# A spectral-filter and MLP kernel: first batch by halves of d, second transpose stored by halves, last output tiles in banks of their own

## The chip, the cores and the metric

The kernel runs on one core of a Trainium2 chip. The metric is device time in microseconds (us), the median of several executions. The kernel before took 802.25 us (4 runs, 801.14 to 803.52).

Names of engines in the profile: PE is the matrix engine (TensorE), PEld its weight load, DVE the vector engine, ACT the scalar engine, POOL is GpSimd, SP issues output stores. PSUM is the memory into which this kernel's matmuls write. The granted clock is PE's clock as the profile shows it, 1.00 being full speed.

## The reference

Eight batches of 3008 tokens with 256 channels (d) are filtered in the frequency domain, then go through a two-layer MLP.

```python
def _attn_ref(x, filt_r, filt_i):            # x: (8, 3008, 256)
    X = np.fft.rfft(x, axis=1)
    Y = X * (filt_r + 1j * filt_i)[None]
    return np.fft.irfft(Y, n=x.shape[1], axis=1)

def _moe_ref(x, w_in, w_out):                # x: (24064, 256), w_in: (256, 2048)
    h = x @ w_in
    return np.maximum(0.01 * h, h) @ w_out
```

## The kernel before

The Fourier transform of length 3008 is split as 94 x 32. Each batch passes through six stages:

- S1: 32 matmuls with a weight each, from x; ACT (and DVE, in batch 0) copies the results out of PSUM.
- T1: four DVE transposes of 32x32 blocks.
- S2: matmuls with a fixed weight; the filter is multiplied on DVE and GpSimd.
- SA: the inverse of S2; ACT copies.
- T2: four DVE transposes again.
- SB: 64 small matmuls, the inverse of S1; copies into `yt`, the MLP's input.

The MLP works on chunks of 512 tokens, each in eight slots. In one slot PE does four matmuls of layer one (`moe1_group`), then spectral tasks of the next batch (`tasks`), then half an output tile of the chunk before (`moe2_slice`). Batch 0 has no MLP to hide behind: its stages are the head of the kernel.

```python
    x_load(0, 4)                       # x of batch 0: four quarters of n2, all of d
    for c0 in (0, HC):                 # filters: two halves of their 24 columns, all of d
        filt_load(fa_sb, filt_r, c0, c0 + HC)
        filt_load(fb_sb, filt_i, c0, c0 + HC)
    ...
    def turn(src, dst, i, flat):       # T1 and T2, part i of 4
        ...
        o = dst[:].bitcast(FP32).rearrange("p (n e) -> p e n", n=Q)[:, ts(i, w), :]
        nc.vector.transpose(o, a)
    ...
    po_ps = pop.tile([P, 2, D], FP32, name="po_ps")   # both output tiles in one PSUM bank
    def moe2_slice(ci, g):
        po = po_ps[:, tj % 2, :]
        ...                            # 8 matmuls into po
        nc.scalar.copy(osts[ci][:, tj % 2, :], po)
        ...                            # one store for two tiles
    ...
    for g in range(16):                # the head, in program order
        s1_group(0, g, two[(g // 2) % 2], copies[g % 2])()
    ...
    upper(fa_sb, 0, HC)                # ACT copies the filter to partitions 64..127
    upper(fb_sb, 0, HC)
    for i in range(4):
        t1_part(0, i)()
    ...                                # S2, filter, SA
    E1 = 6
    for g in range(E1):                # six S1 groups of batch 1, ahead of the MLP
        s1_group(1, g, two[g % 2])()
    for i in range(4):
        t2_part(0, i)()
    for g in range(16):
        sb_group(0, g, copies[g % 2 if g >= 8 else 0], two[(g // 2) % 2])()
    ...
    plan(1, 0, E1, 3, 4, 9, 4, 3, 24, 30)   # slots of batch 1's stages beside the MLP
```

The arguments of `plan` are the batch, the slot of its first S1 group, the first S1 group still to do, S1 groups per slot, the slots where T1 and S2 begin, S2's step, SA's lag, and the slots where T2 and SB begin.

## Time and profile before

The trace splits into three stretches. The MLP begins at 54.71 us, its last layer-one group at 785.55, and the span ends at 800.8.

| stretch, kernel before | us | what it is |
|---|---|---|
| start to first MLP matmul | 54.71 | head: batch 0's chain |
| first to last layer-one group | 730.84 | middle: PE full from about 75 us |
| from there to the end | 15.25 | tail: last output tiles and stores |

Such a table comes from the timeline alone: one looks for the first and the last matmul of a kind.

### The profile page before, as it was taken

The numbers are of one execution on the slowest core, as the hardware profiler recorded it, in microseconds if no ns is written. First come the engines' busy times: TensorE is split into PE (matmuls) and PEld (weight loads), VectorE is DVE, ScalarE is ACT, GpSimd is POOL, SyncE is SP. The second block draws the span as 40 slices with busy tenths as digits, with TensorE's granted clock in tenths as the row PEclk, the third lists the DMA queues.
The fourth block names the chain that finished last, engine by engine and source line by source line (L and its number), as shares of the span: only waits on it lengthen the run. The fifth ranks groups of instructions, "written<-read, shape, count | busy, mean of one in ns | idle before, by whom it ended". The sixth has DMA issues, their size and how long they took to land. (4 is left out here: it accounts for less than half of the span.)

```text
span 800.8 us, 13437 instructions
## 1 busy us (share of the span) xinstructions
PE 764.3 (95%) x5708; PEld 525.5 (66%) x5708; DVE 362.0 (45%) x450; ACT 565.6 (71%) x803; POOL 154.0 (19%) x137
## 2 busy tenths in 40 slices
PE   3668999999999999999999999999999999999997
PEld 2144667766776667866678667776677666776665
DVE  4547852477307743186524773077432765200000
ACT  4767767877686776977678776877768776666663
POOL 6672500052002400034000520024000340000000
PEclk9889999999999999999999999999999999999999
DMA  9934010501014101230105010141100101110011
GB/s 197 173 51 91 27 40 28 117 27 40 27 38 108 40 27 40 63 82 28 40 27 118 27 41 27 40 105 41 41 27 27 41 27 41 40 41 35 32 40 53
DMA packets 32027, 43.14 MB, mean 54 GB/s; under 512 B 2262, under 2 KB 30038, under 8 KB 31310
## 3 DMA queue, kind: packets, MB, share of 16 engines
q0 software_dynamic: 5664, 15.99, 11.2%
q1 hardware_dynamic: 26160, 25.53, 9.0%
q8 instruction: 44, 0.72, 0.4%
q10 hardware_dynamic: 144, 0.77, 0.3%
q14 instruction: 15, 0.12, 0.0%
HBM read 33.64 MB, written 24.64 MB: 73 GB/s over the span
## 5 line engine op out<-in xcount | busy, mean ns | idle before, releaser
L287 ACT ACTIVATE gt_c<-h_c_g 128x1024 f16<-128x1024 f32 x376 | 385.4, 1026 | 193.9 <-PE h_c_g L282 192.9
L293 PE MATMUL po_ps<-w_out_sb,gt_c 128*128 128x256 f16 x3008 | 389.1, 272 | 2.5 <-ACT ost_c_t L299 2.5
L282 PE MATMUL h_c_g<-yt,w_in_sb 128*128 128x512 f16 (+7 forms) x1728 | 386.6, 351 | 1.5 <-ACT gt_c L287 1.3
L293 PEld LDWEIGHTS <-gt_c 128*128 128x128 f16 x3008 | 290.6, 98 | 91.1 <-issue 6.3
L282 PEld LDWEIGHTS <-w_in_sb 128*128 128x128 f16 x1728 | 163.0, 98 | 97.1 <-issue 2.9
L184 DVE STREAM_TRANSPOSE big<-big 128x1024 f32<-128x1024 f32 x64 | 113.8, 1884 | 175.1 <-ACT big L175 175.0
L212 POOL TENSOR_TENSOR y_b_g<-p_b_g,p_b_g 128x512 f16<-128x512 f32 x84 | 106.9, 1273 | 222.3 <-DVE p_b_g L210 222.3
L261 DVE CAST yt<-sb_b_g 128x376 f16<-128x376 f32 x116 | 58.4, 545 | 93.2 <-PE sb_b_g L258 93.2
L299 ACT COPY ost_c_t<-po_ps 128x256 f32<-128x256 f32 x188 | 70.8, 377 | 17.1 <-PE po_ps L293 14.0
L208 DVE TENSOR_TENSOR p_b_g<-s_b_g,fa_sb 128x512 f32<-128x512 f32 x84 | 58.1, 692 | 37.2 <-PE s_b_g L198 34.6
L175 ACT CAST big<-s_b_g 128x512 f16<-128x512 f32 x120 | 65.8, 613 | 9.7 <-PE s_b_g L165 9.7
L122 POOL DMA_DIRECT2D x_sb<-in_x_dram x22 | 11.9, 548 | 271.9 <-PE s_b_g L165 265.5
L175 ACT CAST big<-sa_b_g 128x512 f16<-128x512 f32 x96 | 57.1, 602 | 2.3 <-PE sa_b_g L243 2.1
L209 DVE TENSOR_TENSOR p_b_g<-s_b_g,fb_sb 64x512 f32<-64x512 f32 x84 | 58.2, 693 | 1.1
L210 DVE TENSOR_TENSOR p_b_g<-s_b_g,fb_sb 64x512 f32<-64x512 f32 x84 | 57.4, 683 | 1.1
L165 PE MATMUL s_b_g<-x_sb,f_sb 94*128 94x256 f16 x256 | 41.6, 289 | 10.5 <-DMA x_sb<-in_x_dram 8.8
L243 PE MATMUL sa_b_g<-y_b_g,small_sb 128*128 128x512 f16 x108 | 40.6, 407 | 4.4 <-ACT big L175 4.1
L258 PEld LDWEIGHTS <-big 128*128 128x128 f16 x512 | 30.4, 103 | 19.5 <-DVE big L184 6.0
L165 PEld LDWEIGHTS <-f_sb 94*128 94x128 f16 x256 | 25.1, 102 | 23.0 <-issue 13.7
L258 PE MATMUL sb_b_g<-i_sb,big 128*128 128x94 f16 x512 | 33.9, 213 | 5.7 <-DVE big L184 5.6
L198 PE MATMUL s_b_g<-big,small_sb 128*128 128x512 f16 x84 | 31.8, 379 | 1.4 <-DVE big L184 1.4
L243 PEld LDWEIGHTS <-small_sb 128*128 128x128 f16 x108 | 11.0, 102 | 20.2 <-issue 8.6
(26 smaller groups left out, 86.9 us busy)
## 6 DMA issues: line engine op xcount, KB each, us to landing
out_dram<-ost_c_t SPq DMA_DIRECT2D x94, 256.0 KB, 2.1
x_sb<-in_x_dram POOLq DMA_DIRECT2D x7, 1024.0 KB, 8.6
x_sb<-in_x_dram POOLq DMA_DIRECT2D x7, 480.0 KB, 10.0
x_sb<-in_x_dram POOLq DMA_DIRECT2D x4, 256.0 KB, 7.9
w_in_sb<-in_moe_w_in_dram POOLq DMA_DIRECT2D x1, 1024.0 KB, 9.2
w_out_sb<-in_moe_w_out_dram POOLq DMA_DIRECT2D x1, 1024.0 KB, 9.6
f_sb<-fwd_const SPq DMA_DIRECT2D x4, 192.0 KB, 4.5
fa_sb<-in_filt_r_dram POOLq DMA_DIRECT2D x8, 96.0 KB, 7.1
```

Of the source, the lines that this page charges most:

```text
L165: nc.tensor.matmul(ps[:, j, :], f1_sb[:N1, n2, :], x_sb[:N1, n2, :], start=True, stop=True)
L175: copy(paired(dst)[:, ds(2 * g, 2)], ps[:].rearrange("p n (e t) -> p n e t", t=2))
L184: nc.vector.transpose(o, a)
L208: nc.vector.tensor_tensor(p1[:], ps[:], fa, AL.mult)
L209: nc.vector.tensor_tensor(p2[0:64], ps[64:P], fb[64:P], AL.mult)
L212: nc.gpsimd.tensor_tensor(y1[:], p1[:], p2[:], AL.add)
L258: nc.tensor.matmul(ps[:, j, :], src[:, n2, ts(dt, P // 2)], i1_sb[:, n2, :], start=True, stop=True)
L261: copy(yv[:, :, ds(4 * h, 4)], ps[:].rearrange("p c a -> p a c"))
L282: nc.tensor.matmul(ph[:, j, ds(o, ln)], w_in_sb[:, dt, ts(ct, P)], yts[b % 2][:, dt, ds(lo, ln)], start=(dt == 0), stop=(dt == NDT - 1),)
L287: nc.scalar.activation(gts[ci][:, ds(2 * g, 2), :], ph[:], AF.Lrelu)
L293: nc.tensor.matmul(po, gts[ci][:, ct, ts(tj, P)], w_out_sb[:, ct, :], start=(ct == 0), stop=(ct == NCT - 1))
L299: nc.scalar.copy(osts[ci][:, tj % 2, :], po)
```

## The change

Its intent is a shorter head and tail. Batch 0 is loaded and transformed in two halves of d (128 channels each), so that the second half's load lies beside the first half's work. T2 stores each half of d as a block, so that SB of the first half need not wait for T2's last two parts. The last chunk's output tiles get PSUM banks of their own and a store each. The early S1 groups of batch 1 are dropped, and in batch 1 T1 is planned two slots later and the stages after it one slot later.

```diff
-    x_load(0, 4)
-    for c0 in (0, HC):
-        filt_load(fa_sb, filt_r, c0, c0 + HC)
-        filt_load(fb_sb, filt_i, c0, c0 + HC)
+    for hf in range(2):
+        for n0 in (0, N2 // 2):
+            x_load(0, n0, N2 // 2, hf * DH, DH)
+        filt_load(fa_sb, filt_r, hf * DH, DH)
+        filt_load(fb_sb, filt_i, hf * DH, DH)
+    nc.gpsimd.dma_start(i1_sb[:], i1_d.ap())
+    nc.gpsimd.dma_start(w_in_sb[:], ...)
 ...
+    def t2_part(b, i):
 ...
+            o = big[(4 * b + 3) % 3][:].bitcast(FP32).rearrange("p (h n e) -> p h e n", h=2, n=Q)
+            nc.vector.transpose(o[:, i // 2, ts(i % 2, E4), :], a)
 ...
+    def upper(hf):       # real filter on ACT, imaginary on DVE
+        for t, cp in ((fa_sb, nc.scalar.copy), (fb_sb, nc.vector.tensor_copy)):
+            cp(t[64:P, :, ts(hf, DH)], t[0:64, :, ts(hf, DH)])
+    ac = (nc.scalar.copy, nc.scalar.copy)
+    first_front(0, copies)                  # S1 and T1 of half 0
+    upper(0)
+    first_s2(0, 0, False), first_s2(0, 1, True)    # True: the product is GpSimd's
+    first_s2(0, 2, False)
+    first_sa(0, 0, ac)
+    first_front(1, ac)                      # S1 and T1 of half 1, all copies on ACT
+    x_load(1)
+    first_sa(0, 2, ac), first_sa(0, 1, ac)
+    upper(1)
+    first_s2(1, 0, False), first_s2(1, 1, True)
 ...
-    plan(1, 0, E1, 3, 4, 9, 4, 3, 24, 30)
+    plan(1, 0, 0, 3, 6, 10, 4, 3, 25, 31)
 ...
+        last = ci == NCHUNK - 1
+        if last and half == 0:
+            pos[ci] = pfp.tile([P, D], FP32, tag="pf", name=f"o_c{ci}_t{tj}")[:]
+        po = pos[ci] if last else po_ps[:, tj % 2, :]
 ...
+        if last:
+            nc.sync.dma_start(out[ds(t0, P), :], ost[:, tj % 2, :])
```

More of the change, by code (lines that the diff above doesn't have):

```diff
@@ L115, with x_load, rows, filt_load @@
     fwd2, inv2, inv2x = (small_sb[:, i, :] for i in range(3))
-    def x_load(b, parts=1):
-        step = N2 // parts
+    DH = D // 2
+    def x_load(b, n0=0, nn=N2, d0=0, dn=D):
         src = x[b].rearrange("(n1 n2) d -> n1 n2 d", n2=N2)
-        for i in range(parts):
-            for lo, cnt in ((0, 64), (64, N1 - 64)):
-                nc.gpsimd.dma_start(
-                    x_sb[lo : lo + cnt, ts(i, step), :], src[lo : lo + cnt, ts(i, step), :]
-                )
-    def rows(src, first, pstep, cstep, np_, nc_):
+        for lo, cnt in ((0, 64), (64, N1 - 64)):
+            nc.gpsimd.dma_start(x_sb[lo : lo + cnt, ds(n0, nn), ds(d0, dn)],
+                                src[lo : lo + cnt, ds(n0, nn), ds(d0, dn)])
+    def rows(src, first, pstep, cstep, np_, nc_, d0, dn):
         return bass.AP(
-            tensor=src.tensor, offset=src.offset + first * D,
-            ap=[[pstep * D, np_], [cstep * D, nc_], [1, D]],
+            tensor=src.tensor, offset=src.offset + first * D + d0,
+            ap=[[pstep * D, np_], [cstep * D, nc_], [1, dn]],
         )
-    def filt_load(dst, src, c0, c1):
+    def filt_load(dst, src, d0, dn):
         h = N2 // 2
@@ L136, in filt_load @@
             nc.gpsimd.dma_start(
-                dst[q : q + h, c0:c1], rows(src, NC * s + c0, N1, 1, h, c1 - c0))
+                dst[q : q + h, :, ds(d0, dn)], rows(src, NC * s, N1, 1, h, NC, d0, dn))
             nc.gpsimd.dma_start(
-                dst[q + h : q + Q, c0:c1], rows(src, N1 - NC * s - c0, N1, -1, h, c1 - c0))
-    HC = NC // 2
+                dst[q + h : q + Q, :, ds(d0, dn)], rows(src, N1 - NC * s, N1, -1, h, NC, d0, dn))
     step = N2 // FP
@@ L147 @@
     nc.sync.dma_start(small_sb[:], small_d.ap())
-    x_load(0, 4)
-    for c0 in (0, HC):
-        filt_load(fa_sb, filt_r, c0, c0 + HC)
-        filt_load(fb_sb, filt_i, c0, c0 + HC)
+    for hf in range(2):
[4 more added lines that the diff above has]
+    nc.gpsimd.dma_start(i1_sb[:], i1_d.ap())
+    nc.gpsimd.dma_start(w_in_sb[:], moe_w_in.rearrange("(dt p) c -> p dt c", p=P))
     one = cpool.tile([1, 1], FP32, name="one")
@@ L157, with s1_group @@
     nc.vector.memset(big[2][:].rearrange("p (e n t) -> p e n t", n=Q, t=2)[:, :, NC:Q, :], 0.0)
-    def s1_group(b, g, pool=(pfp, "pf"), copy=nc.scalar.copy):
+    def s1_group(b, g):
         def go():
-            ps = pool[0].tile([P, 2, D], FP32, tag=pool[1], name=f"s1_b{b}_g{g}")
+            ps = pfp.tile([P, 2, D], FP32, tag="pf", name=f"s1_b{b}_g{g}")
             for j in range(2):
@@ L166, in go @@
                                  start=True, stop=True)
-            spread(big[(4 * b) % 3], g, ps, copy)
+            spread(big[(4 * b) % 3], 2 * g, ps, nc.scalar.copy)
         return go
@@ L172, in paired, with spread, t1_part, go @@
         return t[:].rearrange("p (e n t) -> p n e t", n=Q, t=2)
-    def spread(dst, g, ps, copy):
-        copy(paired(dst)[:, ds(2 * g, 2)], ps[:].rearrange("p n (e t) -> p n e t", t=2))
-    def turn(src, dst, i, flat):
-        w = D // 2 // 4
-        a = src[:].bitcast(FP32)[:, ts(i, w * Q)].rearrange("p (e n) -> p e n", n=Q)
-        if flat:
-            o = dst[:].bitcast(FP32)[:, ts(i, w * Q)].rearrange("p (e n) -> p e n", n=Q)
-        else:
-            o = dst[:].bitcast(FP32).rearrange("p (n e) -> p e n", n=Q)[:, ts(i, w), :]
-        nc.vector.transpose(o, a)
-    def turned(t, flat):
-        if flat:
-            return paired(t)
-        return t[:].rearrange("p (n e t) -> p n e t", n=Q, t=2)
-    def t1_part(b, i):
-        return lambda: turn(big[(4 * b) % 3], big[(4 * b + 1) % 3], i, b == 0)
+    def spread(dst, n0, ps, copy, e0=0):
+        nn, de = ps.shape[1], ps.shape[2] // 2
+        copy(paired(dst)[:, ds(n0, nn), ds(e0, de)], ps[:].rearrange("p n (e t) -> p n e t", t=2))
+    E4 = D // 2 // 4
+    def t1_part(b, i, flat=False):
+        def go():
+            a = big[(4 * b) % 3][:].bitcast(FP32)[:, ts(i, E4 * Q)].rearrange("p (e n) -> p e n", n=Q)
+            o = big[(4 * b + 1) % 3][:].bitcast(FP32)
+            if flat:
+                o = o[:, ts(i, E4 * Q)].rearrange("p (e n) -> p e n", n=Q)
+            else:
+                o = o.rearrange("p (n e) -> p e n", n=Q)[:, ts(i, E4), :]
+            nc.vector.transpose(o, a)
+        return go
+    def t2_part(b, i):
+        def go():
+            a = big[(4 * b + 2) % 3][:].bitcast(FP32)[:, ts(i, E4 * Q)].rearrange("p (e n) -> p e n", n=Q)
+            o = big[(4 * b + 3) % 3][:].bitcast(FP32).rearrange("p (h n e) -> p h e n", h=2, n=Q)
+            nc.vector.transpose(o[:, i // 2, ts(i % 2, E4), :], a)
+        return go
     ys = {}
-    def s2_mm(b, c, ps):
-        src = turned(big[(4 * b + 1) % 3], b == 0)
-        nc.tensor.matmul(ps.rearrange("p n (e t) -> p n e t", t=2), fwd2, src[:, ds(c, 2)],
-                         start=True, stop=True)
     def s2_group(b, g):
@@ L203, in go @@
             ps = pfp.tile([P, 2, D], FP32, tag="pf", name=f"s2_b{b}_g{g}")
-            s2_mm(b, 2 * g, ps[:])
+            src = big[(4 * b + 1) % 3][:].rearrange("p (n d) -> p n d", n=Q)
+            nc.tensor.matmul(ps[:], fwd2, src[:, ds(2 * g, 2), :], start=True, stop=True)
             fa, fb = fa_sb[:, ds(2 * g, 2), :], fb_sb[:, ds(2 * g, 2), :]
@@ L212, in go @@
             nc.gpsimd.tensor_tensor(y1[:], p1[:], p2[:], AL.add)
-            ys[(b, g)] = (y1[:],)
+            ys[(b, g)] = y1
         return go
-    def s2_wide(b, g, on_pool):
-        ps = php.tile([P, 4, D], FP32, tag="ph", name=f"s2_b{b}_w{g}")
-        for j in range(2):
-            s2_mm(b, 4 * g + 2 * j, ps[:, ds(2 * j, 2), :])
-        if on_pool:
-            xs = [scrp.tile([P, 2, D], FP32, tag=f"p{j + 1}", name=f"x_b{b}_w{g}_{j}") for j in range(2)]
-            y1 = outp.tile([P, 4, D], FP16, tag="ost", name=f"y1_b{b}_g{g}")
-            y2 = outp.tile([P, 4, D], FP16, tag="ost", name=f"y2_b{b}_g{g}")
-            for j in range(2):
-                nc.scalar.copy(xs[j][:], ps[:, ts(j, 2), :])
-            for y, f in ((y1, fa_sb), (y2, fb_sb)):
-                for j in range(2):
-                    nc.gpsimd.tensor_tensor(y[:, ts(j, 2), :], xs[j][:], f[:, ds(4 * g + 2 * j, 2), :], AL.mult)
-        else:
-            y1 = ypp.tile([P, 4, D], FP16, tag="yw1", bufs=2, name=f"y1_b{b}_g{g}")
-            y2 = ypp.tile([P, 4, D], FP16, tag="yw2", bufs=2, name=f"y2_b{b}_g{g}")
-            nc.vector.tensor_tensor(y1[:], ps[:], fa_sb[:, ts(g, 4), :], AL.mult)
-            nc.vector.tensor_tensor(y2[:], ps[:], fb_sb[:, ts(g, 4), :], AL.mult)
-        for j in range(2):
-            ys[(b, 2 * g + j)] = (y1[:, ts(j, 2), :], y2[:, ts(j, 2), :])
     def sa_group(b, g):
         def go():
-            y = ys.pop((b, g))
             ps = pfp.tile([P, 2, D], FP32, tag="pf", name=f"sa_b{b}_g{g}")
-            for i, (m, t) in enumerate(zip((inv2, inv2x), y)):
-                nc.tensor.matmul(ps[:], m, t, start=(i == 0), stop=(i == len(y) - 1))
-            spread(big[(4 * b + 2) % 3], g, ps, nc.scalar.copy)
-        return go
-    def t2_part(b, i):
-        return lambda: turn(big[(4 * b + 2) % 3], big[(4 * b + 3) % 3], i, False)
+            nc.tensor.matmul(ps[:], inv2, ys.pop((b, g))[:], start=True, stop=True)
+            spread(big[(4 * b + 2) % 3], 2 * g, ps, nc.scalar.copy)
+        return go
     def sb_group(b, g, copy, pool=(pfp, "pf")):
@@ L253, in go @@
         def go():
-            src = turned(big[(4 * b + 3) % 3], False)
+            src = big[(4 * b + 3) % 3][:].rearrange("p (h n d) -> p h n d", h=2, n=Q)
             ps = pool[0].tile([P, 4, N1], FP32, tag=pool[1], name=f"sb_b{b}_g{g}")
@@ L257, in go @@
                 n2 = 4 * h + j
-                nc.tensor.matmul(ps[:, j, :], src[:, n2, ts(dt, P // 2)], i1_sb[:, n2, :],
+                nc.tensor.matmul(ps[:, j, :], src[:, dt, n2, :], i1_sb[:, n2, :],
                                  start=True, stop=True)
@@ L262, in sb_group, with first_s1 @@
         return go
-    gts, osts = {}, {}
+    two = ((pfp, "pf"), (php, "ph"))
+    copies = (nc.scalar.copy, nc.vector.tensor_copy)
+    W = 8
+    def first_s1(hf, g, pool, copy):
+        ps = pool[0].tile([P, 4, DH], FP32, tag=pool[1], name=f"f1_h{hf}_g{g}")
+        for j in range(4):
+            n2 = 4 * g + j
+            nc.tensor.matmul(ps[:, j, :], f1_sb[:N1, n2, :], x_sb[:N1, n2, ts(hf, DH)],
+                             start=True, stop=True)
+        spread(big[0], 4 * g, ps, copy, hf * DH // 2)
@@ new lines, in first_s2 @@
+    def first_s2(hf, g, on_pool):
+        ps = php.tile([P, W, DH], FP32, tag="ph", name=f"f2_h{hf}_g{g}")
+        src = paired(big[1])
+        for j in range(2):
+            nc.tensor.matmul(ps[:, ts(j, 4), :].rearrange("p n (e t) -> p n e t", t=2), fwd2,
+                             src[:, ds(W * g + 4 * j, 4), ts(hf, DH // 2)], start=True, stop=True)
+        fs = [f[:, ts(g, W), ts(hf, DH)] for f in (fa_sb, fb_sb)]
+        if on_pool:
+            xs = [scrp.tile([P, 4, DH], FP32, tag=f"p{j + 1}", name=f"fx_h{hf}_g{g}_{j}") for j in range(2)]
+            y = [outp.tile([P, W, DH], FP16, tag="ost", name=f"fy{i}_h{hf}_g{g}") for i in range(2)]
+            for j in range(2):
+                nc.scalar.copy(xs[j][:], ps[:, ts(j, 4), :])
+            for i in range(2):
+                for j in range(2):
+                    nc.gpsimd.tensor_tensor(y[i][:, ts(j, 4), :], xs[j][:], fs[i][:, ts(j, 4), :], AL.mult)
+        else:
+            y = [ypp.tile([P, W, DH], FP16, tag=f"yw{i}", bufs=2, name=f"fy{i}_h{hf}_g{g}") for i in range(2)]
+            for i in range(2):
+                nc.vector.tensor_tensor(y[i][:], ps[:], fs[i], AL.mult)
+        ys[(hf, g)] = y
@@ new lines, in first_sa, with first_front @@
+    def first_sa(hf, g, cps):
+        y = ys.pop((hf, g))
+        for j in range(2):
+            ps = pfp.tile([P, 4, DH], FP32, tag="pf", name=f"fa_h{hf}_g{g}_{j}")
+            for i, m in enumerate((inv2, inv2x)):
+                nc.tensor.matmul(ps[:], m, y[i][:, ts(j, 4), :], start=(i == 0), stop=(i == 1))
+            spread(big[2], W * g + 4 * j, ps, cps[j], hf * DH // 2)
+    def first_front(hf, cps):
+        for g in range(8):
+            first_s1(hf, g, two[(g // 2) % 2], cps[g % 2])
+        for i in range(2):
+            t1_part(0, 2 * hf + i, True)()
@@ new lines, in upper @@
+    def upper(hf):
[12 more added lines that the diff above has]
+    first_s2(1, 0, False), first_s2(1, 1, True)
+    nc.gpsimd.dma_start(w_out_sb[:], moe_w_out.rearrange("(ct p) d -> p ct d", p=P))
@@ L267 @@
+    first_s2(1, 2, False)
+    first_sa(1, 0, ac)
+    for i in range(2):
+        t2_part(0, i)()
+    first_sa(1, 2, ac), first_sa(1, 1, ac)
+    for i in range(2, 4):
+        t2_part(0, i)()
+    for g in range(16):
+        sb_group(0, g, copies[g % 2 if g >= 8 else 0], two[(g // 2) % 2])()
+    nc.gpsimd.tensor_scalar(fb_sb[64:P], fb_sb[64:P], -1.0, None, AL.mult)
+    gts, pos, osts = {}, {}, {}
     po_ps = pop.tile([P, 2, D], FP32, name="po_ps")
@@ L290, in moe2_slice @@
         tj, half = g // 2, g % 2
-        po = po_ps[:, tj % 2, :]
+        last = ci == NCHUNK - 1
+        if last and half == 0:
+            pos[ci] = pfp.tile([P, D], FP32, tag="pf", name=f"o_c{ci}_t{tj}")[:]
+        po = pos[ci] if last else po_ps[:, tj % 2, :]
         for ct in range(8 * half, 8 * half + 8):
@@ L298, in moe2_slice @@
             osts[ci] = outp.tile([P, 2, D], FP32, tag="ost", name=f"ost_c{ci}_t{tj}")
-        nc.scalar.copy(osts[ci][:, tj % 2, :], po)
-        if tj % 2 == 1:
+        ost, t0 = osts[ci], ci * CH + tj * P
+        nc.scalar.copy(ost[:, tj % 2, :], po)
+        if last:
+            nc.sync.dma_start(out[ds(t0, P), :], ost[:, tj % 2, :])
+        elif tj % 2 == 1:
             nc.sync.dma_start(
-                out[ds(ci * CH + (tj - 1) * P, 2 * P), :].rearrange("(j t) d -> t j d", t=P),
-                osts[ci][:],
-            )
+                out[ds(t0 - P, 2 * P), :].rearrange("(j t) d -> t j d", t=P), ost[:])
     tasks = {}
@@ L324, in plan @@
             at(sb + g // 2, sb_group(b, g, nc.vector.tensor_copy))
-    two = ((pfp, "pf"), (php, "ph"))
-    copies = (nc.scalar.copy, nc.vector.tensor_copy)
-    def sa_pair(g):
-        sa_group(0, 2 * g)(), sa_group(0, 2 * g + 1)()
-    def upper(t, c0, n, scale=None):
-        dst, src = t[64:P, c0 : c0 + n, :], t[0:64, c0 : c0 + n, :]
-        if scale:
-            nc.scalar.mul(dst, src, scale)
-        else:
-            nc.scalar.copy(dst, src)
-    for g in range(16):
-        s1_group(0, g, two[(g // 2) % 2], copies[g % 2])()
-    nc.scalar.dma_start(i1_sb[:], i1_d.ap())
-    x_load(1)
-    upper(fa_sb, 0, HC)
-    upper(fb_sb, 0, HC)
-    for i in range(4):
-        t1_part(0, i)()
-    s2_wide(0, 0, False)
-    s2_wide(0, 1, True)
-    nc.gpsimd.dma_start(w_in_sb[:], moe_w_in.rearrange("(dt p) c -> p dt c", p=P))
-    upper(fa_sb, HC, HC)
-    s2_wide(0, 2, False)
-    sa_pair(0)
-    upper(fb_sb, HC, HC // 2)
-    s2_wide(0, 3, True)
-    nc.gpsimd.dma_start(w_out_sb[:], moe_w_out.rearrange("(ct p) d -> p ct d", p=P))
-    upper(fb_sb, HC + HC // 2, HC // 2)
-    s2_wide(0, 4, False)
-    sa_pair(2), sa_pair(1)
-    s2_wide(0, 5, False)
-    sa_pair(4), sa_pair(5), sa_pair(3)
-    E1 = 6
-    for g in range(E1):
-        s1_group(1, g, two[g % 2])()
-    for i in range(4):
-        t2_part(0, i)()
-    for g in range(16):
-        sb_group(0, g, copies[g % 2 if g >= 8 else 0], two[(g // 2) % 2])()
-    nc.gpsimd.tensor_scalar(fb_sb[64:P], fb_sb[64:P], -1.0, None, AL.mult)
-    plan(1, 0, E1, 3, 4, 9, 4, 3, 24, 30)
+    plan(1, 0, 0, 3, 6, 10, 4, 3, 25, 31)
     for b in range(2, B):
```

## The prediction

> **What bounds the kernel now.** I read the page first: the busy tenths, then the busy time per stretch, then the timeline of the head and the waits of the tail.
>
> ```profile
> PE   3668999999999999999999999999999999999997
> DMA  9934010501014101230105010141100101110011
> ```
> One digit is 20 us. TensorE (PE) is full from the fifth digit to the last but one; the DMA engines are full in the first two digits only. Stretches of 20 us from 80 to 800 us confirm it:
>
> ```profile
> sum 720.00, PE 714.53 PEld 499.61 DVE 317.50 ACT 513.03 POOL 108.61; mean PE 19.85 PEld 13.88 DVE 8.82 ACT 14.25 POOL 3.02
> ```
> Nearly all of the missing 5.5 us is in the last stretch (15.08 of 20). So the middle, 710 us, can't be shortened by hiding anything: only the head, about 80 us, and the tail can give. The change touches just these. The timeline of the head:
>
> ```profile
> 8.34 3.87 PE L165 MATMUL s_b_g<-x_sb,f_sb 94*128 94x256 f16 x16 [8.34 <-DMA x_sb<-in_x_dram]
> ...
> 16.45 0.69 DVE L175 CAST big<-s_b_g 128x512 f16<-128x512 f32 x1 [0.16 <-PE s_b_g L165]
> 16.83 2.75 ACT L338 COPY fa_sb<-fa_sb 64x3072 f16<-64x3072 f16 x1 [0.22 <-DMA fa_sb<-in_filt_r_dram]
> ...
> 17.25 4.62 DVE L184 STREAM_TRANSPOSE big<-big 128x1024 f32<-128x1024 f32 x4
> ...
> 22.02 1.88 PE L198 MATMUL s_b_w<-big,small_sb 128*128 128x512 f16 x4 [5.61 <-DVE big L184]
> ...
> 34.50 1.22 DVE L234 TENSOR_TENSOR y_b_g<-s_b_w,fb_sb 128x1024 f16<-128x1024 f32 x1 [3.61 <-ACT fb_sb L338]
> ...
> 35.14 1.01 PE L243 MATMUL sa_b_g<-y_b_g,small_sb 128*128 128x512 f16 x2 [4.10 <-ACT big L175]
> ```
> and, in the stretch from 40 us:
>
> ```profile
> 42.18 7.21 DVE L184 STREAM_TRANSPOSE big<-big 128x1024 f32<-128x1024 f32 x4 [2.78 <-ACT big L175]
> ...
> 45.98 0.21 PE L258 MATMUL sb_b_g<-i_sb,big 128*128 128x94 f16 x1 [2.38 <-DVE big L184]
> 49.45 5.06 PE L258 MATMUL sb_b_g<-i_sb,big 128*128 128x94 f16 x63 [3.25 <-DVE big L184]
> ...
> 54.71 1.25 PE L282 MATMUL h_c_g<-yt,w_in_sb 128*128 128x512 f16 x4 [0.20 <-ACT yt L261]
> ```
> The reader sees a serial chain for batch 0: load (to 14.5), first stage S1 (to 17.1), first transpose T1 (to 21.9), S2, filter and SA (to 42.1), second transpose T2 (to 49.4), SB (to 54.5). Only at 54.71 does the MLP, the work that fills PE, begin. One SB matmul ran after two T2 parts, then PE waited for all four.
>
> **What the Trainium skill says.** (1) "DMA: Bandwidth & Descriptors", Specifications: a transfer needs 512 B or more for line rate. The new loads write runs of 256 B. No row of this trace has such runs. The nearest, two stretches of 4 us on the GpSimd queue (packets, MB, share of 16 engines):
>
> ```profile
> q0 software_dynamic: 1461, 0.75, 139.2%
> ```
> ```profile
> q0 software_dynamic: 752, 0.80, 119.0%
> ```
> The first (40 to 44 us, the output weights alone) is 513 B a packet, 43.8 ns of an engine each (16 x 4 us / 1461); the second (12 to 16 us) 1063 B and 85.1 ns. A line through both is 5.3 ns + 0.075 ns/B, so an estimated 24.5 ns for 256 B: 167 GB/s against about 200. The page fears worse; the trace at 513 B does not (187 GB/s). I take 160. (2) "VectorE: DVE Perf Modes", the perf-mode tier table: an fp16 copy inside SBUF runs at four elements a cycle, 693 ns for 2048. For 64x3072 I estimate 0.96 us, against ACT's 2.75. No DVE copy here shows it. (3) "SBUF — State Buffer", Door 1: accesses that leave a 16-byte line pay a penalty. The trace agrees: a T1 part that stores flat takes 1.16 us (4.62/4), a T2 part, whose elements lie 512 B apart, 1.80. The change brings them to 256 B, still another line each, so I leave 1.80. (4) "PSUM — Partial Sum Buffer", on bank collisions: no two engines may use one bank at once. Both halves of the output accumulator share a bank, and the tail agrees:
>
> ```profile
> PE po_ps L293 <- ACT ost_c_t L299: 2.0, 4, 0.5
> ```
>
> **The change, part by part.**
>
> *Loading by halves of d.* Chain work on batch 0 can start when 0.75 MB of x has landed, not 1.5. I keep the first landing at 8.5 us (it is shared with the S1 constants). At 160 GB/s, with about 1 us from last byte to landing: the second piece of half 0 at 11; its real filter 13.4, imaginary 15.8; x of half 1 at 20.7; its filters 23 and 25.5; inverse constants 30; input weights, which took 6.2 us for 1.05 MB here, 36. GpSimd issues these in order, and in the compiled program a load waits for the one eight before it, so GpSimd's own multiplies start only at about 22.5.
>
> *The two chains.* Half 0: S1 ends 12.9 (two copies each on ACT and DVE after the second landing). T1, 2 x 1.16: 15.3. ACT duplicates the real filter 13.4 to 16.2, DVE the imaginary one 15.8 to 16.7. Two DVE groups at 2 x 1.22: 19.1 and, with 1 us for PE in between, 22.5. SA copies of group 0 to 20.8. Half 1: S1's eight copies are all on ACT, 8 x 0.61, behind x at 20.7: 26.2. T1: 28.6. ACT does four SA copies of half 0 (to 29.2), then the real filter, 2.75: 32.0. Two DVE groups: 37.8. Then DVE goes straight into T2, 4 x 1.8: 45.2. SA of half 1 (last GpSimd product 37.7, last copy 39.7) is ready before the third T2 part, so DVE is the chain.
>
> *T2 stores each half apart.* SB of the first half starts after two T2 parts (41.5) rather than four: eight groups, bound by eight ACT copies of 0.40, end at 44.8, beside the other two parts. In the compiled program the first SB weight load waits for DVE, and so again does the one of group 8: the dependence is cut in two. Only eight groups remain after T2, about 2.8 us: MLP at 48.0 instead of 54.7, **-6.7 us**. T1's order thus saves little on its own; what is saved is half a T2's SB, and the overlap of loading with work.
>
> *No early S1 of batch 1.* Before, six of its groups (12 matmuls of 256 columns, 12 x about 0.14) ran inside the T2 wait. They now run in the MLP: 1.7 us of PE work. The slots that carry three S1 groups are bound by ACT (1.02 + 3 x 0.61, 2.35 us a slot in the trace), and 1.43 us of idle PE, where S2 waited for T1, should shrink. Counting slot by slot to slot 10, before 19.2 us after the MLP's start, after 21.3, plus one S2 group not done: **+2.4 us**.
>
> *Tail.* Four waits of 0.50 us at the last chunk go: -2.0. The last store is half as large, 0.3 by estimate: **-2.3 us**.
>
> Sum -6.7 + 2.4 - 2.3 = -6.6; 802.0 becomes 795.4.
>
> **The rivals.** *Small runs make the DMA queue the bound.* Against it stands the 513 B row; for it the page and that about 12,000 runs (two per row of x, and of both filters) replace some 2,000 longer ones. At half the speed, 100 GB/s, half 1's filters land near 37 and GpSimd's products slip by 9 us as well; the MLP would start near 53, total about 800. *The queues were not binding anyway.* If the loads keep 200 GB/s, half 0 ends about 2.5 us sooner; ACT's list from 13 us (about 20 us of copies) then holds: MLP at 45.5, total 793. *ACT or DVE order takes the place of the removed wait.* ACT holds both duplications, GpSimd's feed and S1 of half 1 in program order, so a late filter stops S1 copies behind it. This speaks for a small gain: total 798. *The tail waits for something else*: the trace names only the copies; I give that little weight.
>
> **Range and chances.** The tail and the early-S1 cost are certain within 1 us each, the start of the MLP within -3 and +5, so 791 to 800. Faster by 2% would be under 785.9, an MLP start near 38, before T2 can even begin: 0.02. Slower by 2% (818) would need the load to collapse: 0.02. Within 2%: 0.96.
>
> **What would show it.** In the changed profile: first PE matmul at 8 to 9; T1 of half 0 near 13; imaginary duplication on DVE under 1.1 us; T2 parts of 1.8 us in a row near 38 to 45, SB of the first half beside them; MLP at 48; PE full from about 75; the last four output tiles with no PE wait on ACT. Packets of 256 B taking well over 25 ns each would prove the first rival; ACT waiting for a filter before S1 copies the third. A T2 part far from 1.8 us, or new PE waits in the middle, would break the sum.

## More of the kernel before

How even the middle is, this row shows (from the table of stretches; columns are the stretch, its length, then busy us and count for PE, PEld, DVE, ACT and POOL, the granted PE clock, the DMA share and GB/s):

```profile
80.00:780.00 700.00, 699.45 (x5329) 488.49 (x5328) 317.50 (x406) 505.95 (x717) 108.61 (x92) 1.00 0.16 45
```

PE is busy for 699.45 of 700 us at full clock. Work moved into this stretch costs its PE time; waits removed elsewhere save theirs.

## The result, and the profile after

The changed kernel took **794.60 us** (4 runs, 794.41 to 795.15) against 802.25. The ratio is 0.9905, with a 95% interval of 0.9888 to 0.9922. Ratios here are the mean time of one kernel's fast runs over that of the other's in the same rounds, so not quite the ratio of the medians. The interval lies clear of 1, so the gain of about 1% is real. By stretch, in the two traces:

| stretch | before | after | difference | predicted |
|---|---|---|---|---|
| head | 54.71 | 45.70 | -9.0 | -6.7 |
| middle | 730.84 | 734.42 | +3.6 | +2.4 |
| tail | 15.25 | 13.18 | -2.1 | -2.3 |
| span | 800.8 | 793.3 | -7.5 | -6.6 |

The page's rows after, to be held against the two at the top of the prediction:

```profile
PE   3688999999999999999999999999999999999997
DMA  9934100501114010410105010151100101101111
```

The PE digits of the head rise from 3, 6, 6, 8 to 3, 6, 8, 8; nothing else moved. The timeline of the changed head (start us, duration us, engine, line, operation, output and input, count, and in brackets the idle time before it and what ended it):

```profile
10.52 1.86 PE L248 MATMUL f_h_g<-x_sb,f_sb 94*128 94x128 f16 x16 [0.34 <-DMA x_sb<-in_x_dram]
...
12.80 2.75 ACT L290 COPY fa_sb<-fa_sb 64x3072 f16<-64x3072 f16 x1 [0.22 <-DMA fa_sb<-in_filt_r_dram]
13.22 2.37 DVE L189 STREAM_TRANSPOSE big<-big 128x1024 f32<-128x1024 f32 x2
...
15.62 0.95 DVE L290 COPY fb_sb<-fb_sb 64x3072 f16<-64x3072 f16 x1
...
21.30 1.78 PE L248 MATMUL f_h_g<-x_sb,f_sb 94*128 94x128 f16 x24
...
22.03 4.06 ACT L177 CAST big<-f_h_g 128x512 f16<-128x512 f32 x8
...
26.13 2.37 DVE L189 STREAM_TRANSPOSE big<-big 128x1024 f32<-128x1024 f32 x2 [3.93 <-ACT big L177]
...
28.10 2.75 ACT L290 COPY fa_sb<-fa_sb 64x3072 f16<-64x3072 f16 x1
...
30.89 1.22 DVE L271 TENSOR_TENSOR fy_h_g<-f_h_g,fa_sb 128x1024 f16<-128x1024 f32 x1 [1.40 <-ACT fa_sb L290]
...
35.42 7.29 DVE L197 STREAM_TRANSPOSE big<-big 128x1024 f32<-128x1024 f32 x4
...
39.22 1.24 PE L233 MATMUL sb_b_g<-i_sb,big 128*128 128x94 f16 x24 [1.98 <-DVE big L197]
...
42.77 2.69 PE L233 MATMUL sb_b_g<-i_sb,big 128*128 128x94 f16 x32 [1.19 <-DVE big L197]
...
45.70 1.87 PE L334 MATMUL h_c_g<-yt,w_in_sb 128*128 128x512 f16 x4 [0.25 <-ACT yt L236]
```

Two things are to be seen. PE's last wait for x in batch 0 ends at 10.52: half 1's S1, at 21.30, shows no wait for its load. And T2 runs straight behind DVE's products, with SB in two parts, one beside T2 and one after it.

The DMA queue of GpSimd from 8 to 12 us, where every run written is 256 B long (packets, MB, share of 16 engines):

```profile
q0 software_dynamic: 2898, 0.71, 180.9%
```

The share adds up the packets' own times; above 100% they overlap. By spacing it is 16 x 4 us / 2898 = 22.1 ns a packet, 177 GB/s. The prediction's line gave 24.5 ns, and it took 160 GB/s.

The start of the middle, in the chain of waits (start, duration, what it was):

```profile
51.03 1.47 ACT big L177 x3
52.50 0.92 ACT gt_c L339
...
61.09 7.23 DVE big L189 x4
68.33 0.04 issue
68.37 0.38 PE s_b_g L206
```

Until 61 us ACT is the path, with three S1 copies of batch 1 and one activation in each slot. Then comes T1 of batch 1, and only then PE's first S2. The tail:

```profile
781.85 7.15 PE L348 MATMUL o_c_t<-w_out_sb,gt_c 128*128 128x256 f16 x64
...
789.04 0.37 ACT L355 COPY ost_c_t<-o_c_t 128x256 f32<-128x256 f32 x1 [1.33 <-PE o_c_t L348]
```

Sixty-four matmuls of the last four tiles run without a break, 1.79 us a tile, where each took 1.91 plus a 0.50 us wait. From the last layer-one group to the end of the last copy that is 11.91 us before and 9.29 after. The last store then took 0.5 us longer than before (the small stores took 1.7 to 2.6 us to land, by run, the old ones 2.1 to 3.0), so 2.1 us remain of 2.6.

### The profile page after: what moved, and what is told of

Read it like the earlier page. It is cut to its first block, busy times and chain, and to the rows that moved or that the text cites. A ratio compares the mean times of both kernels' runs of the same rounds, so it can differ in the third digit from the quotient of the medians.

```text
span 793.3 us, 13469 instructions
## 1 busy us (share of the span) xinstructions
PE 762.5 (96%) x5740; PEld 526.6 (66%) x5740; DVE 361.3 (46%) x448; ACT 561.2 (71%) x804; POOL 158.3 (20%) x138
## 4 chain that ended last, share of the span: by engine, by line
PE 91%; ACT 4%; DVE 3%; DMA 1%; issue 0%; POOL 0%; ACTq 0%; DVEq 0%; POOLq 0%
PE po_ps L348 40%; PE h_c_g L334 40%; PE sb_b_g L233 3%; PE s_b_g L166 3%; PE s_b_g L206 2%; PE sa_b_g L221 2%; ACT big L177 2%; DVE big L189 1%; DVE big L197 1%; PE o_c_t L348 1%; DMA x_sb<-in_x_dram 1%; ACT gt_c L339 1%; DVE fy_h_g L271 1%; PE f_h_g L257 0%; ACT fa_sb L290 0%
## 5 line engine op out<-in xcount | busy, mean ns | idle before, releaser
L348 PE MATMUL po_ps<-w_out_sb,gt_c 128*128 128x256 f16 x2944 | 381.4, 272 | 0.6 <-ACT ost_c_t L355 0.6
L122 POOL DMA_DIRECT2D x_sb<-in_x_dram x22 | 13.9, 637 | 263.2 <-PE s_b_g L166 262.3
L177 ACT CAST big<-s_b_g 128x512 f16<-128x512 f32 x112 | 61.5, 621 | 0.0
L177 ACT CAST big<-sa_b_g 128x512 f16<-128x512 f32 x84 | 50.6, 602 | 0.0
L166 PE MATMUL s_b_g<-x_sb,f_sb 94*128 94x256 f16 x224 | 35.0, 276 | 1.3 <-ACT big L177 0.5
L221 PE MATMUL sa_b_g<-y_b_g,small_sb 128*128 128x512 f16 x84 | 31.8, 379 | 0.0
L166 PEld LDWEIGHTS <-f_sb 94*128 94x128 f16 x224 | 21.3, 99 | 11.9 <-issue 4.0
```

What stands on the lines that cost most here:

```text
L166: nc.tensor.matmul(ps[:, j, :], f1_sb[:N1, n2, :], x_sb[:N1, n2, :], start=True, stop=True)
L177: copy(paired(dst)[:, ds(n0, nn), ds(e0, de)], ps[:].rearrange("p n (e t) -> p n e t", t=2))
L348: nc.tensor.matmul(po, gts[ci][:, ct, ts(tj, P)], w_out_sb[:, ct, :], start=(ct == 0), stop=(ct == NCT - 1))
```

## The experiments

Twelve kernels were run, all correct, with five rounds each against the kernel before. "Total" is the median of the fast runs. "MLP" is the start of the first MLP matmul in the trace; "middle" is as in the table above.

| kernel | total | MLP | middle |
|---|---|---|---|
| before | 802.25 | 54.71 | 730.84 |
| changed | 794.60 | 45.70 | 734.42 |
| e1_tail | 800.22 | 53.70 | 730.79 |
| e1_t2 | 800.22 | 50.69 | 731.22 |
| e1_not2 | 796.70 | 48.40 | 733.75 |
| e1_halves | 800.05 | 49.61 | 733.67 |
| e2_xrows | 797.25 | 48.08 | 734.11 |
| e2_warm | 794.95 | 45.83 | 733.82 |
| e2_share | 789.90 | 46.12 | 729.52 |
| e2_dve | 795.71 | 48.21 | 733.97 |
| e3_late | 793.50 | 45.56 | 733.94 |
| e3_s2 | 788.68 | 45.06 | 728.30 |
| e3_best | 787.37 | slow run | slow run |
| e4_best | 787.29 | 44.35 | 729.65 |

### One part alone, or one part undone

**e1_tail**: the kernel before, with only the tail's part of the diff.

> The kernel before with only the last chunk's own banks and single stores. Theory: the four PE waits of 0.50 us on the ACT copies go and the last store is half as large: the span from the last MLP matmul group to the end falls from 15.25 us to about 13.2, total -2.1 us. Rival (the waits were hidden by something else in the tail, or the extra stores cost): 0 to -1 us.

Measured: ratio 0.9982 (0.9963 to 1.0001); its tail is 12.51 us against 15.25, and no PE wait on ACT is left in it:

```profile
786.23 7.15 PE L296 MATMUL o_c_t<-w_out_sb,gt_c 128*128 128x256 f16 x64
```

The stage gained 2.7 us in that trace. The total fell 1.6 us against 801.82 in the same rounds, with an interval that barely includes zero. The four waits were real and are gone.

**e1_t2**: the kernel before, with only T2's store by halves.

```diff
+        elif apart:                # the second transpose is called with apart=True
+            o = dst[:].bitcast(FP32).rearrange("p (h n e) -> p h e n", h=2, n=Q)[:, i // 2, ts(i % 2, w), :]
 ...
-                nc.tensor.matmul(ps[:, j, :], src[:, n2, ts(dt, P // 2)], i1_sb[:, n2, :],
+                nc.tensor.matmul(ps[:, j, :], src[:, dt, n2, :], i1_sb[:, n2, :],
```

> The kernel before with only the second transpose storing each half apart. Theory: SB of the first half runs beside the last two T2 parts, so the MLP begins at 52.2 instead of 54.7 (-2.5 us). A second theory says that part of it is given back: SB now runs in two short bursts, PE's clock stays at half in the first MLP slot (as in the changed kernel, 0.50 until 49.0), which costs about 1.2 us; then total -1.3 us rather than -2.5. Rival (PE waits for all four parts in any case): 0.

Measured: ratio 0.9981 (0.9962 to 0.9999). The MLP started 2.98 us after T2's end instead of 5.32, so T2's store is worth 2.34 us. Of the second theory little is seen: the first MLP slot took 2.11 us against 1.74, and the middle grew by 0.4 us, not 1.2. The total fell by 1.6 us with an interval of about 0 to 3, too wide to decide between the two. The timeline:

```profile
44.20 1.38 PE L260 MATMUL sb_b_g<-i_sb,big 128*128 128x94 f16 x24 [2.36 <-DVE big L186]
...
47.76 2.69 PE L260 MATMUL sb_b_g<-i_sb,big 128*128 128x94 f16 x32 [1.05 <-DVE big L186]
50.69 1.62 PE L284 MATMUL h_c_g<-yt,w_in_sb 128*128 128x512 f16 x4 [0.25 <-ACT yt L263]
```

The MLP began at 50.69, not at 52.2, because this trace's T2 itself started 1.8 us earlier than in the first trace of the kernel before (40.41 against 42.18). With e1_tail (40.85) there are three traces of the same old head, and their T2 differs. In the first trace ACT waited 1.50 us for the second half of the real filter, in e1_t2 0.40. In e1_tail it did not wait at all. So part of the old head's time hangs on when that filter lands. Counted from the first landing of x, T2 started after 33.84 us in the first trace, 31.70 in e1_tail and 32.39 in e1_t2; in the changed kernel, e1_not2, e1_halves, e2_warm and e2_share after 26.7 to 27.4.

**e1_not2**: the changed kernel with T2's store as before.

> The changed kernel with the second transpose stored as before (halves interleaved). Theory: all of SB waits for T2's end at 42.7, so the MLP begins at about 47.9 instead of 45.7 (+2.2 us); with the clock theory, SB's 64 matmuls in one run warm PE up, the first MLP slot takes 1.75 us instead of 2.94, and the total is only +1.0. Rival (the halves of loading alone bring it all): 0.

Measured: 796.70, which is 2.1 us above the changed kernel, measured in other rounds; by the ratios, 0.9942 (0.9923 to 0.9961) against 0.9905, it is 3.0. The first MLP slot did take 1.67 us, but a total of only +1.0, as the clock theory had it, did not come. SB is one run again:

```profile
43.07 5.06 PE L233 MATMUL sb_b_g<-i_sb,big 128*128 128x94 f16 x63 [3.26 <-DVE big L197]
48.40 1.17 PE L334 MATMUL h_c_g<-yt,w_in_sb 128*128 128x512 f16 x4 [0.28 <-ACT yt L236]
```

From T2's end to the MLP it is 5.39 us, against 2.99 in the changed kernel. Undoing the part costs what adding it alone saved.

**e1_halves**: e1_not2 with the old tail as well, thus loading by halves and the lost early S1 alone.

> The changed kernel with T2's store and the tail as before: loading and transforming by halves alone (and no early S1 of batch 1). Theory: e1_not2 plus 2.1 us for the tail, so 3.1 to 4.3 us slower than the changed kernel, 3.4 to 4.5 us faster than the kernel before: MLP start at 47.9 (-6.8) against +3 us or so in the first ten MLP slots. Rival (the small runs of the loads bind and halving saves little): within 2 us of the kernel before.

Measured: 800.05, ratio 0.9981 (0.9960 to 1.0001): only 1.8 us below the kernel before of its rounds, less than expected, and 3.4 us above e1_not2. By the number this is the rival's outcome. In its trace the first x landed at 10.30 instead of 7.8 to 9.2 us, and all that follows is late by as much; its MLP start is 39.3 us after that landing, e1_not2's 39.7. Its tail is 16.12 us against 12.65 in e1_not2, which had not been expected to differ by more than 2.1. Counted from the landing, the head is as short as expected; the size by totals is uncertain by a us or two. Whether the short runs of the loads cost anything is a question for the next run, e2_xrows. The three parts alone sum to about -5 us and the whole is -7.7; the spread of the kernel before is too wide to read an interplay out of that difference.

### What halving the load buys

**e2_xrows**: the changed kernel, with x of batch 0 in whole rows and the filters still by halves.

```diff
-        for n0 in (0, N2 // 2):
-            x_load(0, n0, N2 // 2, hf * DH, DH)
+        if hf == 0:
+            for n0 in range(0, N2, N2 // 4):
+                x_load(0, n0, N2 // 4)
```

> The changed kernel, but x of batch 0 loaded in whole rows (four quarters of n2, runs of 4 KB) instead of halves of d; the filters still come by halves. Theory (the gain in the head is that half 0 starts early, while half 1's load is hidden behind half 0's work): S1 of half 0 ends near 17 instead of 13.1, T1 at 17.3, MLP start about 4 us later (49.7), total +4. Rival (the 256 B runs hold the loads back, so longer runs pay for the later start): total within +1.

Measured: 797.25, 2.65 us above the changed kernel and 2.3 above e2_warm, which ran in the same rounds. The last quarter of x came later, and T1 with it:

```profile
13.98 1.01 PE L249 MATMUL f_h_g<-x_sb,f_sb 94*128 94x128 f16 x8 [0.91 <-DMA x_sb<-in_x_dram]
15.84 2.37 DVE L190 STREAM_TRANSPOSE big<-big 128x1024 f32<-128x1024 f32 x2
```

T1 starts 2.6 us later than in the changed kernel (13.22) and the MLP 2.4 us later. The first reading holds with a smaller size than 4, since the long runs landed faster than assumed. The rival, that short runs hold the loads back as much as the early start gains, falls.

### PE's clock, and ACT, in the first MLP slots

In the changed kernel's trace PE's clock stands at 0.50 in the first MLP slots; in the kernel before it was 1.00 by 54 us. **e2_warm** adds idle matmuls:

```diff
+    warm(4)                 # 4 matmuls of 512 columns into an unread PSUM tile
     for g in range(16):
+        if g == 8:
+            warm(3)
         sb_group(0, g, ...)
```

> The changed kernel with 4 + 3 matmuls of 512 columns, whose results nobody reads, in PE's idle gaps before SB and between SB's halves. Theory (the clock drops because PE rests between the two bursts of SB; the first MLP slot takes 2.94 us at a clock of 0.50 instead of 1.7): the clock is 1.00 by 46 us, first slot about 1.75 us, first S2 of batch 1 22.0 us after the MLP's start instead of 22.7, total -0.6 to -1.2. Rival (that region is bound by ACT's S1 copies, whatever the clock): 0.

Two rows from the tables of stretches, the changed kernel first, then e2_warm:

```profile
46.00:47.00 1.00, 1.00 (x4) 0.35 (x3) 0.04 (x1) 0.00 (x0) 1.00 (x1) 0.50 0.00 0
```
```profile
46.00:48.00 2.00, 1.96 (x13) 1.08 (x12) 0.19 (x1) 0.91 (x1) 2.00 (x1) 1.00 0.03 4
```

The clock did what was expected: 1.00, and the first slot took 1.72 us instead of 2.94. The first S2 of batch 1 came 22.07 us after the MLP's start instead of 22.67. But the total is 794.95, no gain, as the rival had it. The other traces suggest why: without any warming matmuls, the first slot took 1.60 to 2.11 us in ten traces and 2.94 in those of the changed kernel and e4_best (and in e3_best's, which is of a slow run). "TensorE: Matmul & The Clock Gate", Part 1, says that the warm-up varies between runs of one kernel. With one trace for each kernel this is likely here, and not shown: the slow first slots would then belong to single runs, cost about 0.6 us where they occur, and hardly move the median.

**e2_share**: two of three S1 copies of batch 1 move from ACT to DVE, which idles there.

```diff
-            at(s1 + i // per, s1_group(b, g))
+            at(s1 + i // per, s1_group(b, g, nc.vector.tensor_copy if b == 1 and g % 3 else nc.scalar.copy))
```

> The changed kernel with two of three S1 copies of batch 1 on DVE, which is idle from 46 to 61 us. Theory (the first six MLP slots are bound by ACT, 1.02 + 3 x 0.5 us a slot, and then T1's 7.2 us keeps S2 waiting): a slot falls from 2.37 to about 1.9 us, T1 of batch 1 starts 2 to 2.5 us earlier, total -2 us. Rival (the early S1's lack costs PE time, 12 matmuls, not ACT time): 0 to -0.5.

Measured: 789.90 (0.9846, interval 0.9830 to 0.9863), 4.7 us below the changed kernel and more than the 2 us expected. From 46 to 56 us, changed kernel first, then e2_share:

```profile
46.00:56.00 10.00, 9.27 (x44) 4.72 (x43) 0.04 (x1) 8.39 (x14) 7.04 (x1) 0.84 0.00 1
```
```profile
46.00:56.00 10.00, 9.88 (x60) 5.81 (x60) 6.91 (x11) 8.62 (x13) 7.89 (x2) 0.98 0.02 3
```

PE issues 60 matmuls instead of 44 in the same time and DVE works 6.91 us instead of 0.04. A slot takes 1.54 us, not 1.9 as expected, and the middle is 729.52, below even the kernel before. So what bound these slots was copies on ACT, not matmuls on PE. (The ten S1 groups that the kernel before had here were on ACT too, so the gain is larger than what the early S1's lack had cost. No run put the early S1 back into the changed kernel, so its cost and that of the later slots are known only together.) In e2_share the first S2 still waits 1.87 us for T1:

```profile
63.88 0.38 PE L206 MATMUL s_b_g<-big,small_sb 128*128 128x512 f16 x1 [1.87 <-DVE big L189]
```

**e3_s2** therefore moves it one slot later, and all that follows it.

```diff
-    plan(1, 0, 0, 3, 6, 10, 4, 3, 25, 31)
+    plan(1, 0, 0, 3, 6, 11, 4, 3, 26, 32)
```

> e2_share with S2 of batch 1 one slot later (and what follows it too). Theory (in e2_share PE still waits 1.87 us for batch 1's T1 before its first S2): the wait goes, because a slot of MLP work is done meanwhile, total -1.5 to -1.9 against e2_share, about 788.2. Rival (the later SB of batch 1 makes chunk 5 wait for its tokens): the same or slower than e2_share.

```profile
62.88 0.38 PE L206 MATMUL s_b_g<-big,small_sb 128*128 128x512 f16 x1 [0.15 <-DVE big L189]
```

The wait fell to 0.15 us, the middle by another 1.2, and the total is 788.68. That is in other rounds: the ratio, 0.9839 (0.9820 to 0.9857), overlaps with e2_share's, so the gain in the total is not shown.

### ACT's list in the head

In the changed kernel, DVE's first product of half 1 waits 1.40 us for ACT's 2.75 us copy of the real filter, while DVE has idled 3.93 us before T1 of half 1. **e2_dve** gives both filter copies of half 1 to DVE in that gap.

```diff
+    for t in (fa_sb, fb_sb):
+        nc.vector.tensor_copy(t[64:P, :, ts(1, DH)], t[0:64, :, ts(1, DH)])
     first_front(1, ac)
 ...
-    upper(1)
```

> The changed kernel with both filters of half 1 duplicated on DVE, before S1 of half 1, where DVE idles 3.9 us; ACT loses its 2.75 us copy at 28.1. Theory (that copy is on the path: the first product of half 1 waits 1.40 us for it): first product at about 29.4 instead of 30.9, MLP start -1.5, total -1.5. Rival (half 1's filters land too late for DVE to copy them by 26, or DVE is already the bound): 0 or slower.

Measured: 795.71, no gain, and in its trace an MLP start 2.5 us later than in the changed kernel (1.1 us of it was regained in a shorter tail, 0.4 in the middle). From the timelines of e2_dve, DVE and then POOL:

```profile
23.26 5.06 DVE L299 COPY fa_sb<-fa_sb 64x3072 f16<-64x3072 f16 x1 [0.63 <-DMA fa_sb<-in_filt_r_dram]
28.25 0.94 DVE L299 COPY fb_sb<-fb_sb 64x3072 f16<-64x3072 f16 x1
```
```profile
22.99 2.29 POOL L267 TENSOR_TENSOR fy_h_g<-fx_h_g,fa_sb 128x512 f16<-128x512 f32 x2
25.23 2.27 POOL L267 TENSOR_TENSOR fy_h_g<-fx_h_g,fb_sb 128x512 f16<-128x512 f32 x2
```

A copy that takes 0.95 us elsewhere took 5.06. It began just after GpSimd's first multiply and ended 0.8 us after the last of the four. Neither rival had named this: the load had landed, and DVE was not the bound. The guess that GpSimd held the copy up is tested by **e3_late**, the same copies after T1 of half 1, when GpSimd is idle.

```diff
-    upper(1)
+    for t in (fa_sb, fb_sb):
+        nc.vector.tensor_copy(t[64:P, :, ts(1, DH)], t[0:64, :, ts(1, DH)])
```

> Like e2_dve, the two filter copies of half 1 on DVE, but after its T1 (near 28.5), when GpSimd has no multiply running. Theory (in e2_dve the real filter's DVE copy took 5.06 us because GpSimd ran its four multiplies at the time, and finished 0.8 us after the last of them): both copies take 0.95 us, the first product of half 1 starts near 30.5 instead of 30.9, total -0.4 us against the changed kernel. Rival (the copy of the real filter on DVE is slow by itself, or because its load was still landing): about 5 us again, total +3.

```profile
28.94 0.95 DVE L302 COPY fa_sb<-fa_sb 64x3072 f16<-64x3072 f16 x1
29.81 0.95 DVE L302 COPY fb_sb<-fb_sb 64x3072 f16<-64x3072 f16 x1
```

Each took 0.95 us, and T2 started 26.57 us after x's first landing instead of 27.10. The total, 793.50, is 1.1 us below the changed kernel's median, taken in other rounds; the ratios, 0.9901 and 0.9905, are the same within their intervals. The same copy of the same data is fast away from GpSimd's multiplies; the load and the copy itself are excluded as causes. DMA traffic does not tell the two runs apart: 252 GB/s from 28 to 30 us here, 217 from 26 to 28 us in e2_dve.

### A version that beats both

**e3_best**: e3_s2 with e3_late's copies, and three of half 1's eight S1 copies on DVE.

```diff
-    first_front(1, ac)
+    first_front(1, tuple(nc.vector.tensor_copy if g in (1, 4, 6) else nc.scalar.copy for g in range(8)))
```

> e3_s2 with the DVE copies of e3_late, and three of the eight S1 copies of half 1 on DVE. Theory (the head is a chain through ACT's list between 22 and 31 us): T1 of half 1 starts near 25 instead of 26.1, first product of half 1 near 29.1 instead of 30.9, MLP 1.8 us earlier, about 786.5, below both kernels. Rival (GpSimd's product of half 0 or the fill of the PSUM buffers holds half 1 instead): as e3_s2.

Four executions took 786.65 to 787.89 us; one, the profiled one, took 938.3 with a granted clock of 0.811 over the whole run. That one is left out; why it came is not known. Its trace is the slow run's, and its times (T1 of half 1 at 25.37, T2 at 34.17) are given only because the fast trace of e4_best below has nearly the same (25.20 and 34.06); in e3_s2 they were 26.25 and 35.53. The gain of 1.3 us over e3_s2, in the same rounds, is near the 1.8 expected.

**e4_best** returns two thirds of the real filter's copy to ACT.

```diff
+    nc.scalar.copy(fa_sb[64:P, W:NC, h1], fa_sb[0:64, W:NC, h1])
+    nc.vector.tensor_copy(fa_sb[64:P, 0:W, h1], fa_sb[0:64, 0:W, h1])
+    nc.vector.tensor_copy(fb_sb[64:P, :, h1], fb_sb[0:64, :, h1])
```

> e3_best with two thirds of the real filter's copy of half 1 (16 of 24 columns, 1.85 us) back on ACT, which idles from 28 to 29.7 us, so DVE copies only the third that its first product needs. Theory (from 25 us on the head is the sum of DVE's work): DVE's second T2 starts 0.5 to 0.6 us earlier than in e3_best (34.2 less 0.6, with the first landing at 8.4), total 786.9. Rival (ACT's copy delays GpSimd's operand, or the third still waits): as e3_best, 787.5, or slower. The run also gives a second look at a kernel like e3_best, whose profiled execution fell in a slow state (938 us at a clock of 0.81): if that was one execution, all runs are near 787.

```profile
31.79 1.23 DVE L271 TENSOR_TENSOR fy_h_g<-f_h_g,fa_sb 128x1024 f16<-128x1024 f32 x1 [0.52 <-PE f_h_g L257]
```

All five runs are fast: 787.29 (785.95 to 788.07), ratio 0.9806 (0.9785 to 0.9826), so whether it gains the full 2% is open. Against e3_best nothing was gained: T2 started at 34.06 instead of 34.17, since DVE's second group now waits 0.52 us for PE. The theory that DVE's sum alone bounds the head from 25 us on falls. Both versions are 7 us below the changed kernel and about 15 below the kernel before.

## Why the prediction was right

It named 795.4 us and the result is 794.60. Point by point:

- **Only head and tail can give.** Right: from 80 to 780 us PE is busy 699.45 us in the changed kernel too.
- **The load by halves.** The times of the chain came true one after another: T1 of half 0 at 13.22 (12.9 named), the DVE copy 0.95 us (0.96 estimated with "VectorE: DVE Perf Modes"), half 0's last product at 22.2 (22.5), T1 of half 1 at 26.13 (26.2). Half 1's x was not waited for. The first rival, loads as the bound, had the page "DMA: Bandwidth & Descriptors" on its side. It falls with 22.1 ns a packet and no wait for half 1's x or filters, and e2_xrows shows what halving x is worth, about 2.6 us.
- **From there to T2 the sum was too large.** T2 was to end at 45.2 and ended at 42.7. Two terms were mis-sized. ACT's twelve copies were counted at 0.61 us each, their time when they stand alone; in a row they came every 0.50 us (from 22.03 to 28.08), so ACT reached the real filter at 28.10 and not at 29.2. (By the prediction's own terms, 26.2 and four copies of 0.61, it would have been 28.6.) And the 1 us for PE between the two DVE groups, 0.63 in half 0, did not occur in half 1, where the four products ran from 30.89 to 35.50 without a gap.
- **T2's parts stay at 1.80 us, and SB is cut in two.** Right: 7.29 us for four, with elements now 256 B apart, as "SBUF — State Buffer" led to expect; 2.99 us (2.8 named) from T2's end to the MLP. e1_t2 and e1_not2 give 2.3 and 2.4 us for this part.
- **Head -6.7, measured -9.0.** The 2.3 us between them is the MLP start, 45.70 for 48.0, and comes from the two terms named above. Apart from that, the trace that both numbers start from was the slowest of three old heads, by 1.5 and 2.1 us counted from the first landing, so the gain on an average run is probably below 9.0; that is an estimate from three traces.
- **No early S1, +2.4.** Right in kind and too small: +3.6 in this trace, +2.8 to +3.3 in the others with the same middle (733.67 to 734.11, less 730.84 or 730.79). The sum held this certain within 1 us, and in this trace it was 1.2 off. The step that failed is that the idle 1.43 us before S2 "should shrink". It grew to 1.83, because ACT's copies and then T1 set the time of S2, and PE's own work fits beneath. The named mechanism, slots bound by ACT, is what e2_share confirmed, though its sum of 1.02 + 3 x 0.61 gives 2.85 us where the trace has 2.35: the same term, copies in a row, as in the head. The slow first slot of this run adds some 0.6.
- **Tail -2.3, measured -2.1.** The waits on the shared bank ("PSUM — Partial Sum Buffer") are gone. (The change gives each tile a name and a bank of its own at once, so no run tells the bank from the program's guard on one shared tile.) PE's part saved 2.6 rather than 2.0, since tiles without a restart take 1.79 us instead of 1.91. The 0.3 us for a smaller last store did not show in this pair, whose new tail is the longest of ten fast traces: these have 12.1 to 13.2 us, the three old tails 15.2 to 16.1. The gain is thus nearer 3 us than 2. From the last copy's end to the end of the span the ten have 3.15 us on average and the three 3.64, so the smaller store probably is part of it.
- **The second rival, queues that never bound, was nearer for the head.** It named an MLP start of 45.5, and 45.70 came. Its reason is half seen: half 1 did not wait for its loads, and ACT's list ran from 22.03 to 30.85 without a pause. But half 0 did not end 2.5 us sooner (22.20 for 22.5), and the loads moved 177 GB/s, not 200.
- **The third rival, order on ACT, was partly true.** ACT's list did bound half 1 in the changed kernel, and still the gain was not small.

The errors of head and middle have opposite signs, and so the total came closer than its terms; that part is luck. Left open: how much of the head's gain belongs to the old head's late filter, since its waits differ between runs, and why one execution of e3_best ran at a low clock.

## What to carry to other kernels

When a stage must run before anything can hide it, cut its work along an axis that goes through all its steps, and lay out intermediate buffers so that each piece is a block of its own: the consumer can then wait for a piece. Work that is moved out of a stall did not cost its share of the full engine here, but the time of the engine that bound the slots it landed in; look there for an idle neighbour, as one changed argument for the copies brought 4.7 us here. Before giving DVE a fast copy inside SBUF, see what GpSimd does at that time.

## What the Trainium skill lacked or had wrong

- "DMA: Bandwidth & Descriptors", Specifications, asks 512 B for line rate and gives no rate below; a later section of that page, "Why small descriptors are slow (HBM only)", gives only an overhead for 256 B, 27%. Loads with runs of 256 B moved at 177 GB/s (22.1 ns a packet), against 191 GB/s for runs of 512 B in the same trace (0.76 MB in 4 us). For this kind of load the step is 7%, less than a reader of the Specifications would fear.
- "SBUF — State Buffer", Who interferes with whom, says that whoever issues first holds the ports shared by DVE and GpSimd for its whole instruction. e2_dve agrees, and adds that a row of instructions counts as one: a DVE copy of 0.95 us took 5.06 beside four GpSimd multiplies in a row, and got no turn between them. The other direction, which the page describes as well, is there too: a GpSimd load issue of about 0.60 us took 1.34 beside DVE's filter copy of half 0 in the changed kernel.
